# Attention backward on one Trainium2 core: score, dP and dQ matmuls interleaved by head, operands stored by group of heads, and a start flag in place of dQ's memset

## The chip, the cores and the metric

The kernel runs on one core of one Trainium2 chip. The metric is the device time of one execution in microseconds (us); medians of several executions are quoted.

PE is the matmul engine, DVE the vector engine, ACT the activation engine, POOL and SP the two engines that issue most transfers. The kernel uses PSUM as eight banks of 2 KB per partition (its pools take 8 of 8, below); PE writes there, DVE and ACT read from there. The trace records the clock granted to PE: at half clock, matmuls of 512 columns start about 0.41 us apart here in place of 0.215.

## The reference, cut to what matters

One block of a diffusion-style transformer, forward and backward, with S = 2048 tokens, D = 512, and attention with 32 heads of 16.

```python
def _A_ref(x, wqkv, wo):                      # attention
    H = 32; Dh = D // H
    qkv = (x @ wqkv).reshape(B, S, 3, H, Dh).transpose(2, 0, 3, 1, 4)
    q, k, v = qkv[0], qkv[1], qkv[2]
    p = softmax(einsum('bhqd,bhkd->bhqk', q, k) * Dh ** -0.5)
    o = einsum('bhqk,bhkd->bhqd', p, v)
    return o.transpose(0, 2, 1, 3).reshape(B, S, D) @ wo
...
h = layernorm(x) * (1 + ca) + sa
x = x + ga * _A_ref(h, A_wqkv, A_wo)
h = layernorm(x) * (1 + cb) + sb
x = x + gb * mlp(h)                           # squared relu, F = 1792
# outputs: x and the gradients of nine inputs for a given grad_out
```

For each head, the backward pass needs dV = P^T dO', dS = P * (dP - delta), dQ = dS K and dK = dS^T Q, where P is the softmax, recomputed. The kernel divides dO by the softmax sum beforehand (dO') and writes minus delta into padding columns of dO', so that dS is exp(score) times dP as PE delivers it.

## The kernel before: the parts that matter

The heads go in 8 groups of 4, each in 2 pairs. A pair has 4 chunks of 512 keys times 16 blocks of 128 queries: 64 units, 1024 in all. A unit makes two score matmuls, two dP matmuls, two exps, one multiplication (`ds`), and, later, its share of dQ, dK and dV. Every four units one DMA transpose of dS is issued, 256 in all; dQ needs its result two groups later.

```python
stp  = tile_pool(name="p5st", bufs=2, space=PSUM)   # score: 2 banks
dpp  = tile_pool(name="p5dp", bufs=2, space=PSUM)   # dP: 2 buffers of 2 banks
acckv, accq                                         # dK/dV and dQ: 1 bank each, 8 of 8 in use
...
def load_group(g):                                  # operands of the next 4 heads, at the group's turn
    for n, src in {"QT": QTq_d, "dOT": dOTq_d}.items():        # feature-major, 512 KB each
        nc.gpsimd.dma_start(t[:], src[g])
    for n, src in {"K": ktm_d, "Q": qtm_d, "dO": dOp_d}.items():  # token-major, 256 KB each, [S, D] in memory
        nc.gpsimd.dma_start(t[:], src.rearrange("(st p) d -> p st d", p=P)[:, :, g * W:(g + 1) * W])

def dq(u):
    if c == 0 and ib == 0:
        nc.vector.memset(accq[:], 0.0)              # once per pair
    for a in range(2):
        for sub in range(4):
            nc.tensor.matmul(accq[:, ib, a, :], lhsT=dsT[...], rhs=T["K"][...], start=False, stop=False)
    if c == SC - 1 and ib == ST - 1:
        nc.vector.tensor_scalar(d, accq[:], self.scale, None, ALU.mult)   # copy dQ out
...
for i in range(G):                                  # G = 4 units
    for a in range(2): matmul(sts[a], QT, masked KT)           # two scores
    if turnq and i == 3: turn(...)                  # once per pair: dK/dV transposed through a dP buffer
    for a in range(2): matmul(dp[:, a], dOT, masked VT)        # two dP
    for a in range(2): activation(pu[:, a], sts[a], Exp)
    nc.vector.tensor_tensor(dsg[:, i], dp[:], pu[:], ALU.mult)
    if len(pendq) > 2 * G: dq(pendq.pop(0))         # dQ of an earlier unit
    if i == 1: kv_group()                           # dK/dV of four earlier units
nc.sync.dma_start_transpose(dsT[:], dsg[...])
```

The softmax here doesn't subtract the row's maximum and nothing guards it: scores larger than these inputs give would overflow.

Of the kernel before, what the change touches and what calls it, by code (L numbers as in the profile page):

```python
# [33 lines left out]
class K:  # L34
# [29 lines left out]
    def build(self, ctx: ExitStack):  # L64
        tc, nc = self.tc, self.nc
        self.dram_pool = ctx.enter_context(tc.tile_pool(name="dram", bufs=1, space=DRAM))
        self.pp = ctx.enter_context(tc.tile_pool(name="persist", bufs=1))
        S, D, F, H, NQ, ST, DT, FT = self.S, self.D, self.F, self.H, self.NQ, self.ST, self.DT, self.FT
        self.xhat1_d = self.dram("xhat1_d", [S, D], BF16)
        self.qtm_d = self.dram("qtm_d", [S, D], BF16)  # L70
        self.ktm_d = self.dram("ktm_d", [S, D], BF16)
        self.QTq_d = self.dram("QTq_d", [NQ, P, S], BF16)
        self.KTq_d = self.dram("KTq_d", [NQ, P, S], BF16)
        self.VTq_d = self.dram("VTq_d", [NQ, P, S], BF16)
        self.dOTq_d = self.dram("dOTq_d", [NQ, P, S], BF16)
        self.O_d = self.dram("O_d", [S, D], BF16)
        self.O32_d = self.dram("O32_d", [S, D], F32)
        self.xhat2_d = self.dram("xhat2_d", [S, D], BF16)
        self.rT_d = self.dram("rT_d", [FT, P, S], BF16)
        self.duT_d = self.dram("duT_d", [FT, P, S], BF16)  # L80
        self.dx1_d = self.dram("dx1_d", [S, D], F32)
        self.vaug_d = self.dram("vaug_d", [P, ST * H * (DH + 1)], BF16)
        self.dOp_d = self.dram("dOp_d", [S, D], BF16)
        self.dqkv_d = self.dram("dqkv_d", [S, 3 * D], BF16)
        self.dx1b_d = self.dram("dx1b_d", [S, D], BF16)
        self.stash = False
        if self.stash:
            self.put_d = self.dram("put_d", [NQ * 2 * self.SC * ST, P, 2, 512], BF16)

        stop = self.opts.get("stop_after", 99)  # L90
        self.dmaq = [nc.gpsimd]
        self.dmai = 0
        self.open_pools = {}
        phases = [self.phase0, self.phase12, self.phase12b, self.phase3, self.phase4, self.phase45, self.phase5, self.phase6, self.phase7]
        for i, ph in enumerate(phases):
            ph()
            if stop <= i:
                break
        for name in list(self.open_pools)[::-1]:
            self.close_pool(name)  # L100
# [153 lines left out]
    def phase12(self):  # L254
# [8 lines left out]
        with tc.tile_pool(name="p12", bufs=1) as sb, tc.tile_pool(name="p12e", bufs=8) as eb:  # L263
# [11 lines left out]
            qtm_v = self.qtm_d.rearrange("(st p) d -> p st d", p=P)  # L275
            ktm_v = self.ktm_d.rearrange("(st p) d -> p st d", p=P)
# [16 lines left out]
            def tm_group(ps_pool, st, t):  # L293
# [4 lines left out]
                if t < 2:  # L298
# [4 lines left out]
                    dq.dma_start((qtm_v if t == 0 else ktm_v)[:, st, :], ev[:])  # L303
# [76 lines left out]
            with tc.tile_pool(name="p2c", bufs=1) as cp, tc.tile_pool(name="p2q", bufs=2) as qp, \  # L380
# [56 lines left out]
                nc.gpsimd.dma_start(self.O_d.rearrange("(st p) d -> p st d", p=P), O_tm[:])  # L437

# [477 lines left out]
    def step_5a(self, wk, trps, ps, st, dx1_f32):  # L916
# [24 lines left out]
        nc.gpsimd.dma_start(self.dOp_d.rearrange("(st p) d -> p st d", p=P)[:, st, :], dOp_t[:])  # L941
# [133 lines left out]
    def attn_bwd(self):  # L1075
# [11 lines left out]
        with ExitStack() as es:  # L1087
# [20 lines left out]
            def load_group(g):  # L1108
# [5 lines left out]
                for n, src in tm.items():  # L1114
                    t = qp.tile([P, ST, W], BF16, name=f"{n}g")
                    with nc.allow_non_contiguous_dma(reason="128B runs"):
                        nc.gpsimd.dma_start(t[:], src.rearrange("(st p) d -> p st d", p=P)[:, :, g * W:(g + 1) * W])
                    T[n] = t
# [23 lines left out]
            def dq(u):  # L1142
                (T, g, jp, c, ib, i, dsT) = u
                if c == 0 and ib == 0:
                    nc.vector.memset(accq[:], 0.0)
                for a in range(2):
                    col = (2 * jp + a) * DH
                    for sub in range(4):
                        nc.tensor.matmul(accq[:, ib, a, :], lhsT=dsT[:, (i * 2 + a) * 4 + sub, :],  # L1149
                                         rhs=T["K"][:, 4 * c + sub, col:col + DH], start=False, stop=False,  # L1150
                                         skip_group_check=True)
                if c == SC - 1 and ib == ST - 1:
# [14 lines left out]
            turnq = []  # L1167
            with tc.manual_schedule(engines={mybir.EngineType.PE}):
                for g in range(NQ):
                    Tn = load_group(g + 1) if g + 1 < NQ else None  # L1170
                    for jp in range(2):
# [3 lines left out]
                        for c in range(SC):  # L1175
                            c0 = 512 * c
                            for ib0 in range(0, ST, G):
                                dsg = dsp.tile([P, G, 2, 512], BF16, name="ds")
                                for i in range(G):
                                    ib = ib0 + i  # L1180
                                    q = slice(ib * P, (ib + 1) * P)
                                    sts = [stp.tile([P, 512], F32, name="st") for a in range(2)]
                                    for a in range(2):
                                        nc.tensor.matmul(sts[a][:], lhsT=T["QT"][:, q], rhs=masked["KT"][2 * jp + a][:, c0:c0 + 512],  # L1184
                                                         start=True, stop=True)
                                    if turnq and i == 3:
                                        turn(*turnq.pop(0))
                                    dp = dpp.tile([P, 2, 512], F32, name="dp")
                                    for a in range(2):
                                        nc.tensor.matmul(dp[:, a, :], lhsT=T["dOT"][:, q], rhs=masked["VT"][2 * jp + a][:, c0:c0 + 512],  # L1190
                                                         start=True, stop=True)
                                    pu = pup.tile([P, 2, 512], BF16, name="pu")
                                    for a in range(2):
                                        nc.scalar.activation(pu[:, a, :], sts[a][:], ACT.Exp, scale=self.scale)  # L1194
                                    nc.vector.tensor_tensor(dsg[:, i], dp[:], pu[:], ALU.mult)  # L1195
                                    pend.append((T, g, jp, c, ib, kvT, pu, dsg[:, i]))
                                    if len(pendq) > 2 * G:
                                        dq(pendq.pop(0))
# [10 lines left out]
                while pendq:  # L1209
                    dq(pendq.pop(0))  # L1210
# [264 lines left out]
```

## Time and profile before

| | before |
|---|---|
| median of four executions (lowest to highest) | 3472.1 us (3465.1 to 3480.0) |
| attention backward, first to last dS transpose | 1624.1 us |
| median distance of dS transposes | 5.857 us |
| excess: the distances' sum over 255 times the median | 130.5 us |
| PE busy share of the whole span | 87% |

Two views more are worth having. The first is the page's list of costly groups: line, engine, operation, output and inputs, count, busy us, mean ns of one, and the idle time just before them with what ended most of it.

```profile
L1194 ACT ACTIVATE pu<-st 128x512 bf16<-128x512 f32 x2048 | 1101.7, 595 | 508.3 <-PE st L1184 506.5
L1195 DVE TENSOR_TENSOR ds<-dp,pu 128x1024 bf16<-128x1024 f32 x1024 | 1211.0, 1220 | 366.4 <-ACT pu L1194 269.2
L1184 PE MATMUL st<-KTm,QTq 128*128 128x512 bf16 x2048 | 698.5, 384 | 58.2 <-DMA dOTq<-dOTq_d 7.1
L1190 PE MATMUL dp<-VTm,dOTq 128*128 128x512 bf16 x2048 | 617.2, 383 | 0.1
```

ACT and DVE have hundreds of microseconds of idle time here and PE has little, so PE's order is what they wait for. Note the dP matmuls: before the change PE never waited for a dP buffer (0.1 us).

The second view is PE in order of time around a pair boundary (start, length, engine, operation; x2 is two in a row).

```profile
1971.13 0.60 PE L1127 MATMUL acckv<-ds,Qg 128*16 128x512 bf16 x2
1971.52 0.64 PE L1127 MATMUL acckv<-ds,Qg 128*16 128x512 bf16 x2
...
1977.78 0.39 PE L1127 MATMUL acckv<-ds,Qg 128*16 128x512 bf16 x2
1977.99 0.38 PE L1127 MATMUL acckv<-ds,Qg 128*16 128x512 bf16 x2
```

Just after the memset's wait the dK/dV matmuls start about 0.4 us apart; one group later, 0.21. This wait costs its own length and then 3.4 us at half clock. One of the 15 pair boundaries separates the two: at 2998 us the same wait of 2.8 us is followed by full clock, and that boundary loses 2.7 us at the memset, not 4.2.

### The profile page before, as it was taken

Reading aid. Unit: us, or ns where it says so; the run is one execution under the profiler, and the core shown is the slowest. Engines: PE = TensorE matmul, PEld = TensorE weight load, DVE = VectorE, ACT = ScalarE, POOL = GpSimd, SP = SyncE. Lnnn points to the kernel's source line nnn. Section 1 sums busy time; section 2 is a strip of 40 time slices with the busy share of each in tenths; the row PEclk is TensorE's granted clock in tenths of the full one; section 3 lists DMA queues with packets and bytes.
Section 4 is the critical chain, followed back from the end, with each engine's and each line's share of the span. In section 5 each row is a group of like instructions: output and inputs, shape, how many; then the busy total and the mean of one; then the engine's idle time right before and its main releaser. Section 6 shows DMA issues by size and latency. Waiting matters only on the chain. (4 is left out here: it accounts for less than half of the span.)

```text
span 3465.0 us, 75624 instructions
## 1 busy us (share of the span) xinstructions
PE 2998.7 (87%) x31556; PEld 1452.4 (42%) x31556; DVE 1876.3 (54%) x2761; ACT 2350.4 (68%) x3577; POOL 369.9 (11%) x583
## 2 busy tenths in 40 slices
PE   5999998888885968498998989989899998999887
PEld 2445543333332433265443444444344444444433
DVE  6222220000004346364886778878677787887755
ACT  3999999999992324332776667667676676776633
POOL 3111110000002004231101010010101001000000
PEclk8999999999997989699999999999999999999998
DMA  3111110000004365654999999999999999999952
GB/s 123 62 49 50 45 41 12 12 6 12 5 1 164 105 206 196 179 150 117 198 176 172 174 189 178 176 176 175 174 175 184 183 176 176 177 175 172 179 182 66
DMA packets 1178339, 447.82 MB, mean 129 GB/s; under 512 B 1089162, under 2 KB 1145612, under 8 KB 1177996
## 3 DMA queue, kind: packets, MB, share of 16 engines
q1 hardware_dynamic: 1140188, 353.70, 53.1%
q0 software_dynamic: 29184, 79.59, 7.9%
q10 hardware_dynamic: 8624, 9.70, 0.9%
q8 instruction: 247, 4.05, 0.5%
q14 instruction: 96, 0.79, 0.1%
HBM read 106.83 MB, written 67.64 MB: 50 GB/s over the span
## 5 line engine op out<-in xcount | busy, mean ns | idle before, releaser
L1194 ACT ACTIVATE pu<-st 128x512 bf16<-128x512 f32 x2048 | 1101.7, 595 | 508.3 <-PE st L1184 506.5
L1195 DVE TENSOR_TENSOR ds<-dp,pu 128x1024 bf16<-128x1024 f32 x1024 | 1211.0, 1220 | 366.4 <-ACT pu L1194 269.2
L412 ACT ACTIVATE pu<-st 128x1024 bf16<-128x1024 f32 x1024 | 940.1, 1381 | 4.7 <-PE accbank L418 4.7
L1184 PE MATMUL st<-KTm,QTq 128*128 128x512 bf16 x2048 | 698.5, 384 | 58.2 <-DMA dOTq<-dOTq_d 7.1
L1190 PE MATMUL dp<-VTm,dOTq 128*128 128x512 bf16 x2048 | 617.2, 383 | 0.1
L409 PE MATMUL st<-QTm,KTq 128*128 128x512 bf16 x2048 | 606.9, 377 | 6.3 <-ACT pu L412 1.5
L1149 PEld LDWEIGHTS <-dsT 128*128 128x128 bf16 x8192 | 354.4, 96 | 343.1 <-issue 57.1
L418 PEld LDWEIGHTS <-pu 128*128 128x128 bf16 x8192 | 291.9, 96 | 457.9 <-ACT pu L412 407.4
L1149 PE MATMUL accq<-Kg,dsT 128*128 128x16 bf16 x8192 | 356.3, 170 | 92.4 <-DMA dsT<-ds 50.0
L418 PE MATMUL accbank<-Vaug,pu 128*128 128x17 bf16 x8192 | 353.9, 172 | 67.3 <-DVE accbank L405 7.4
L1190 PEld LDWEIGHTS <-dOTq 128*128 128x128 bf16 x2048 | 199.7, 98 | 377.5 <-issue 199.0
L427 DVE RECIPROCAL rl<-accbank 128x4 f32<-128x4 f32 x128 | 23.0, 179 | 526.1 <-PE accbank L418 525.6
L1127 PE MATMUL acckv<-ds,Qg 128*16 128x512 bf16 x2048 | 280.3, 398 | 0.6 <-DVE ds L1195 0.6
L1127 PE MATMUL acckv<-pu,dOg 128*16 128x512 bf16 x2048 | 280.3, 398 | 0.0
L458 POOL DMA_DIRECT2D KTm<-KTq_d x120 | 59.6, 501 | 1151.6 <-PE st L1184 1151.4
L1184 PEld LDWEIGHTS <-QTq 128*128 128x128 bf16 x2048 | 123.0, 96 | 128.9 <-issue 127.3
L288 DVE TENSOR_SCALAR ev_fm<-pps,bcol 128x512 bf16<-128x512 f32 x92 | 69.1, 751 | 195.0 <-PE pps L281 194.0
L409 PEld LDWEIGHTS <-KTq 128*128 128x128 bf16 x2048 | 130.0, 96 | 34.8 <-issue 20.5
L281 PE MATMUL pps<-xhat1T,wpad 128*128 128x512 bf16 x384 | 122.8, 378 | 4.9 <-DVE ev_fm L288 3.8
L1127 PEld LDWEIGHTS <-Qg 128*16 128x16 bf16 x2048 | 75.8, 89 | 73.4 <-issue 12.7
L1127 PEld LDWEIGHTS <-dOg 128*16 128x16 bf16 x2048 | 75.6, 89 | 0.0
L545 ACT ACTIVATE rT<-ups,bias 128x512 bf16<-128x512 f32 x56 | 38.5, 687 | 52.1 <-PE ups L543 52.0
(305 smaller groups left out, 2376.1 us busy)
## 6 DMA issues: line engine op xcount, KB each, us to landing
rT_d<-rT SPq DMA_DIRECT2D x4, 1792.0 KB
rT<-rT_d SPq DMA_DIRECT2D x4, 1792.0 KB
duT_d<-duT POOLq DMA_DIRECT2D x4, 1792.0 KB, 12.9
rT_f<-rT_d SPq DMA_DIRECT2D x14, 512.0 KB
duT_f<-duT_d POOLq DMA_DIRECT2D x14, 512.0 KB, 4.0
xhat_d<-xhat SPq DMA_DIRECT2D x2, 2048.0 KB
QTq_d<-ev_fm POOLq DMA_DIRECT2D x32, 128.0 KB, 2.1
QTm<-QTq_d SPq DMA_DIRECT2D x128, 32.0 KB
```

Of the source, the lines that this page charges most:

```text
L281: nc.tensor.matmul(pt[:, :sw], lhsT=wpads[t][:, kt, g, :], rhs=xhat1T[:, kt, s0:s0 + sw], start=(kt == 0), stop=(kt == DT - 1))
L288: nc.vector.tensor_scalar(ev[:, :sw], pt[:, :sw], bc, None, ALU.add)
L409: nc.tensor.matmul(stt[:, a, :qw], lhsT=KT[:, kb * P:(kb + 1) * P], rhs=QTm[a][:, q0:q0 + qw], start=True, stop=True)
L412: nc.scalar.activation(pu[:, :, :qw], stt[:, :, :qw], ACT.Exp, scale=self.scale)
L418: nc.tensor.matmul(acc[:, a, sub, :], lhsT=pu[:, a, sub * P:(sub + 1) * P], rhs=Vaug[:, kb, heads[a], :], start=False, stop=False, skip_gr ...
L458: eng.dma_start(masked[n][j][r:r + 32, c0:c0 + cw], src[g, r:r + 32, c0:c0 + cw])
L1127: nc.tensor.matmul(acckv[r:r + DH, :], lhsT=T[n][:, ib, col:col + DH], rhs=src[:, a, :], start=(ib == 0), stop=(ib == ST - 1))
L1149: nc.tensor.matmul(accq[:, ib, a, :], lhsT=dsT[:, (i * 2 + a) * 4 + sub, :], rhs=T["K"][:, 4 * c + sub, col:col + DH], start=False, stop=F ...
L1184: nc.tensor.matmul(sts[a][:], lhsT=T["QT"][:, q], rhs=masked["KT"][2 * jp + a][:, c0:c0 + 512], start=True, stop=True)
L1190: nc.tensor.matmul(dp[:, a, :], lhsT=T["dOT"][:, q], rhs=masked["VT"][2 * jp + a][:, c0:c0 + 512], start=True, stop=True)
L1194: nc.scalar.activation(pu[:, a, :], sts[a][:], ACT.Exp, scale=self.scale)
L1195: nc.vector.tensor_tensor(dsg[:, i], dp[:], pu[:], ALU.mult)
```

## The change

The intent has three parts. (1) Each score matmul is followed by the dP matmul of the same head and its part of dQ, so that ACT has time to empty a score bank. (2) The token-major operands K, Q and dO are stored by group of heads, so that a later load reads 2 KB runs in place of 128 B runs; the stores then write 128 B runs. (3) dQ's first matmul of a pair carries a start flag, so the memset, which had to wait for the copy of the pair before, goes; dQ work of the new pair is held back for two units (`hold`), and done in doubles later.

```diff
-        self.qtm_d = self.dram("qtm_d", [S, D], BF16)          # also ktm_d, dOp_d
+        self.qtm_d = self.dram("qtm_d", [NQ, P, ST * 4 * DH], BF16)
...
+    def by_quad(self, t):
+        return t.rearrange("g p (st w) -> p st g w", st=self.ST)
...
-        nc.gpsimd.dma_start(self.dOp_d.rearrange("(st p) d -> p st d", p=P)[:, st, :], dOp_t[:])
+            nc.gpsimd.dma_start(self.by_quad(self.dOp_d)[:, st], dOp_t[:].rearrange("p (g w) -> p g w", g=NQ))
...
-                        nc.gpsimd.dma_start(t[:], src.rearrange("(st p) d -> p st d", p=P)[:, :, g * W:(g + 1) * W])
+                    nc.gpsimd.dma_start(t[:].rearrange("p st w -> p (st w)"), src[g])
...
-                if c == 0 and ib == 0:
-                    nc.vector.memset(accq[:], 0.0)
-                for a in range(2):
+                for a in heads:
...
-                                         rhs=T["K"][:, 4 * c + sub, col:col + DH], start=False, stop=False,
+                                         rhs=T["K"][:, 4 * c + sub, col:col + DH],
+                                         start=(c == 0 and ib == 0 and a == 0 and sub == 0), stop=False,
...
+                                    if len(pendq) > 2 * G:
+                                        if pendq[0][3] == 0 and pendq[0][4] == 0 and hold:
+                                            hold -= 1
+                                        else:
+                                            hold = 2 if pendq[0][4] else 0
+                                            uqs = [pendq.pop(0) for _ in range(2 if len(pendq) > 3 * G - i else 1)]
...
                                     for a in range(2):
+                                        nc.tensor.matmul(stt[:], lhsT=T["QT"][:, q], rhs=masked["KT"][...], start=True, stop=True)
+                                        nc.scalar.activation(pu[:, a, :], stt[:], ACT.Exp, scale=self.scale)
                                         nc.tensor.matmul(dp[:, a, :], lhsT=T["dOT"][:, q], rhs=masked["VT"][...], start=True, stop=True)
+                                        for uq in uqs:
+                                            dq(uq, [a])
```

More of the change, by code (lines that the diff above doesn't have):

```diff
@@ L69, in build @@
         self.xhat1_d = self.dram("xhat1_d", [S, D], BF16)
-        self.qtm_d = self.dram("qtm_d", [S, D], BF16)
-        self.ktm_d = self.dram("ktm_d", [S, D], BF16)
+        self.qtm_d = self.dram("qtm_d", [NQ, P, ST * 4 * DH], BF16)
+        self.ktm_d = self.dram("ktm_d", [NQ, P, ST * 4 * DH], BF16)
         self.QTq_d = self.dram("QTq_d", [NQ, P, S], BF16)
@@ L82, in build @@
         self.vaug_d = self.dram("vaug_d", [P, ST * H * (DH + 1)], BF16)
-        self.dOp_d = self.dram("dOp_d", [S, D], BF16)
+        self.dOp_d = self.dram("dOp_d", [NQ, P, ST * 4 * DH], BF16)
         self.dqkv_d = self.dram("dqkv_d", [S, 3 * D], BF16)
@@ L274, in phase12 @@
             dsts = [self.QTq_d, self.KTq_d, self.VTq_d]
-            qtm_v = self.qtm_d.rearrange("(st p) d -> p st d", p=P)
-            ktm_v = self.ktm_d.rearrange("(st p) d -> p st d", p=P)
+            qtm_v = self.by_quad(self.qtm_d)
+            ktm_v = self.by_quad(self.ktm_d)
             def fm_group(ps_pool, t, g, s0, sw, eng="vector"):
@@ L302, in tm_group @@
                     self.dmai += 1
-                    dq.dma_start((qtm_v if t == 0 else ktm_v)[:, st, :], ev[:])
+                    with nc.allow_non_contiguous_dma(reason="128B runs"):
+                        dq.dma_start((qtm_v if t == 0 else ktm_v)[:, st], ev[:].rearrange("p (g w) -> p g w", g=NQ))
                 else:
@@ L940, in step_5a @@
                                 self.rl[:, st, :].unsqueeze(2).to_broadcast([P, H, DH]), ALU.mult)
-        nc.gpsimd.dma_start(self.dOp_d.rearrange("(st p) d -> p st d", p=P)[:, st, :], dOp_t[:])
+        with nc.allow_non_contiguous_dma(reason="128B runs"):
+            nc.gpsimd.dma_start(self.by_quad(self.dOp_d)[:, st], dOp_t[:].rearrange("p (g w) -> p g w", g=NQ))
         prod = wk.tile([P, H, DH], F32, name="prod")
@@ L1115, in load_group @@
                     t = qp.tile([P, ST, W], BF16, name=f"{n}g")
-                    with nc.allow_non_contiguous_dma(reason="128B runs"):
-                        nc.gpsimd.dma_start(t[:], src.rearrange("(st p) d -> p st d", p=P)[:, :, g * W:(g + 1) * W])
+                    nc.gpsimd.dma_start(t[:].rearrange("p st w -> p (st w)"), src[g])
                     T[n] = t
@@ L1140, in turn, with dq @@
                     nc.scalar.copy(d, v[:, t, :, :, 0:DH])
-            def dq(u):
+            def dq(u, heads):
                 (T, g, jp, c, ib, i, dsT) = u
-                if c == 0 and ib == 0:
-                    nc.vector.memset(accq[:], 0.0)
-                for a in range(2):
+                for a in heads:
                     col = (2 * jp + a) * DH
@@ L1149, in dq @@
                         nc.tensor.matmul(accq[:, ib, a, :], lhsT=dsT[:, (i * 2 + a) * 4 + sub, :],
-                                         rhs=T["K"][:, 4 * c + sub, col:col + DH], start=False, stop=False,
+                                         rhs=T["K"][:, 4 * c + sub, col:col + DH],
+                                         start=(c == 0 and ib == 0 and a == 0 and sub == 0), stop=False,
                                          skip_group_check=True)
-                if c == SC - 1 and ib == ST - 1:
+                if c == SC - 1 and ib == ST - 1 and 1 in heads:
                     h0 = 4 * g + 2 * jp
@@ L1166, in attn_bwd @@
             T = load_group(0)
-            turnq = []
+            turnq, hold = [], 0
             with tc.manual_schedule(engines={mybir.EngineType.PE}):
@@ L1181, in attn_bwd @@
                                     q = slice(ib * P, (ib + 1) * P)
-                                    sts = [stp.tile([P, 512], F32, name="st") for a in range(2)]
-                                    for a in range(2):
-                                        nc.tensor.matmul(sts[a][:], lhsT=T["QT"][:, q], rhs=masked["KT"][2 * jp + a][:, c0:c0 + 512],
-                                                         start=True, stop=True)
+                                    uqs = []
+                                    if len(pendq) > 2 * G:
[4 more added lines that the diff above has]
+                                            uqs = [pendq.pop(0) for _ in range(2 if len(pendq) > 3 * G - i else 1)]
                                     if turnq and i == 3:
@@ L1188, in attn_bwd @@
                                     dp = dpp.tile([P, 2, 512], F32, name="dp")
+                                    pu = pup.tile([P, 2, 512], BF16, name="pu")
                                     for a in range(2):
+                                        stt = stp.tile([P, 512], F32, name="st")
+                                        nc.tensor.matmul(stt[:], lhsT=T["QT"][:, q], rhs=masked["KT"][2 * jp + a][:, c0:c0 + 512],
+                                                         start=True, stop=True)
+                                        nc.scalar.activation(pu[:, a, :], stt[:], ACT.Exp, scale=self.scale)
                                         nc.tensor.matmul(dp[:, a, :], lhsT=T["dOT"][:, q], rhs=masked["VT"][2 * jp + a][:, c0:c0 + 512],
                                                          start=True, stop=True)
-                                    pu = pup.tile([P, 2, 512], BF16, name="pu")
-                                    for a in range(2):
-                                        nc.scalar.activation(pu[:, a, :], sts[a][:], ACT.Exp, scale=self.scale)
+                                        for uq in uqs:
+                                            dq(uq, [a])
                                     nc.vector.tensor_tensor(dsg[:, i], dp[:], pu[:], ALU.mult)
                                     pend.append((T, g, jp, c, ib, kvT, pu, dsg[:, i]))
-                                    if len(pendq) > 2 * G:
-                                        dq(pendq.pop(0))
                                     if i == 1 and len(pend) >= G + 2:
@@ L1209, in attn_bwd @@
                 while pendq:
-                    dq(pendq.pop(0))
+                    dq(pendq.pop(0), [0, 1])
     def phase6(self):
```

## The prediction

> **What bounds the kernel now.** I cut the span by stage first, with the view of busy time in stretches. One stage is over half of it: the backward pass through attention, from 1560 to 3330 us.
>
> ```profile
> 1560.00:3330.00 1770.00, 1596.92 (x17510) 780.02 (x17509) 1319.32 (x1205) 1142.60 (x2101) 157.07 (x279) 0.96 0.98 175
> ```
>
> The columns are the stretch, its length, busy us of PE, PE weight loads, DVE, ACT, POOL, the granted clock, the DMA share and GB/s. PE is busy 90% of it and the DMA engines 98%, so a busy share doesn't say which one sets the end. The whole change lies in this stage, apart from the stores that feed it. I then read the waits inside it, 1700 to 3300 us:
>
> ```profile
> ACT pu L1194 <- PE st L1184: 494.0, 506, 10.2
> DVE ds L1195 <- ACT pu L1194: 256.2, 272, 2.4
> PE accq L1149 <- DMA dsT<-ds: 50.0, 7, 9.8
> PE accq L1149 <- DVE accq L1145: 42.4, 15, 3.0
> ```
>
> PE itself is named with few waits: 50 us for transposed dS to land, once per group of heads, and 42 us for the memset of dQ, once per pair. To see the rest I read one regular group of four units (a unit is one query block of a head pair) in order of time:
>
> ```profile
> 2213.31 0.59 PE L1190 MATMUL dp<-VTm,dOTq 128*128 128x512 bf16 x2
> 2213.74 0.35 PE L1149 MATMUL accq<-Kg,dsT 128*128 128x16 bf16 x8
> 2213.94 0.86 PE L1184 MATMUL st<-KTm,QTq 128*128 128x512 bf16 x2
> 2214.41 4.75 DVE L1195 TENSOR_TENSOR ds<-dp,pu 128x1024 bf16<-128x1024 f32 x4 [1.10 <-ACT pu L1194]
> ...
> 2215.28 0.59 PE L1184 MATMUL st<-KTm,QTq 128*128 128x512 bf16 x2
> ...
> 2216.34 0.86 PE L1184 MATMUL st<-KTm,QTq 128*128 128x512 bf16 x2
> 2216.83 0.31 PEld L1190 LDWEIGHTS <-dOTq 128*128 128x128 bf16 x2 [0.39 <-issue]
> ```
>
> The two score matmuls take 0.59 us in one unit and 0.86 in the next. The 0.27 us more is a wait: there are two score banks, and the second matmul waits until ACT has read its bank. PE counts as busy in it. The groups follow each other every 5.857 us (the median distance between the starts of the 256 dS transposes). PE alone needs 5.31: four units of 1.065 (2215.276 to 2216.341 holds no wait) plus 1.047 for the dK/dV matmuls with their gaps. So PE order and two waits of 0.27 set the pace. The transposes do not:
>
> ```profile
> L1204 SPq DMA_TRANSPOSE dsT<-ds x256: 4764/5042/14930, 1652.0 to 3276.1; - x128
> ```
>
> They run one at a time, 5.04 us in the median, 0.8 less than the period.
>
> The 255 periods sum to 1624.1 us, 130.5 over 255 times the median. Sorted by place, that excess is: about 1.0 us per pair at the turn of dK/dV; 4.2 us at 15 pair boundaries (63 us), where the memset is; and about 9 us more at each of the six boundaries before which a new group's operands load (55 us).
>
> **What the Trainium skill says.** "TensorE: Matmul & The Clock Gate", section "Wait — 56ns, not 53.3ns?", gives 215.7 ns between warm matmuls of 512 columns and a floor near 25 ns for small ones. The trace agrees: 0.215 us for score and dP, 0.0255 for one dQ matmul, weight loads hidden. Its section "What's actually happening" says that PE drops to half clock after an idle window of about 3.4 us. The trace agrees: PE starts nothing for 3.16 us at the memset, and the next dK/dV matmuls come 0.41 us apart, not 0.215. That explains why a wait named at 2.8 us costs 4.2. "PSUM — Partial Sum Buffer", section "The four PSUM rules", says that a first matmul clears the written-bits of its whole 2 KiB bank, and later ones overwrite where the bit is clear. dQ's accumulator is 16 x 2 x 16 floats, one bank, so one start flag can replace the memset; this trace can't show it. "DMA: Bandwidth & Descriptors", section "Specifications", asks for 512 B per transfer for line rate. The trace fits that:
>
> ```profile
> QTq<-QTq_d POOLq DMA_DIRECT2D x6, 512.0 KB, 5.4
> dOTq<-dOTq_d POOLq DMA_DIRECT2D x6, 512.0 KB, 6.9
> ...
> Qg<-qtm_d POOLq DMA_DIRECT2D x6, 256.0 KB, 14.9
> dOg<-dOp_d POOLq DMA_DIRECT2D x6, 256.0 KB, 14.8
> ```
>
> Half the bytes, in 128 B runs, take over twice the time to land. One dS transpose took 14.9 us beside them.
>
> **The change part by part.**
>
> *Interleaving.* No matmul or weight load is added. Each unit becomes score, dP, four dQ matmuls for head 0, then the same for head 1. A half is 0.215 + 0.215 + 4 x 0.0255 = 0.532 us. A score bank is busy 0.412 (matmul start to exp start) + 0.592 (exp) + 0.052 (release) = 1.056 us and is wanted every 2 x 0.532 = 1.064, so both 0.27 us waits go. But dP has two buffers too, and its loop grows. Call D the start of a unit's first dP matmul. Now the second score matmul comes before D, and ds starts 1.10 us after D (2213.306 to 2214.407), runs 1.222 and releases 0.054 later (the latency that PE shows after the memset): 2.38 us. In the new order the second score matmul starts at D + 0.317, so ds starts at D + 0.317 + 0.412 + 0.594 + 0.032 = D + 1.355 and the buffer is free at D + 2.63. The next use is two units on, after 2 x 1.065 = 2.13 us of PE. Where the dK/dV matmuls lie between, nothing waits; where they don't, the first dP waits 0.50. The unit after waits 0.08, because ds follows ds at 1.141 us. New group: 5.31 + 0.58 = 5.89 us, against 5.857. Over 256 groups **+9 us**: a wait on ACT is swapped for a wait on DVE.
>
> *Memset.* 15 boundaries lose 4.2 us. What remains is the copy of dQ out of its bank (0.68 us), which stands on DVE ahead of the last ds of its group. Two units without dQ let it finish; the double ones after them spend that PE time again. I leave 0.6 us: 15 x 3.6 = **-54 us**.
>
> *The turn.* Its transposes take one of the dP buffers, whose loop now binds; I carry the recurrence above through it and get 1.9 us where there was 1.0: 16 x 0.9 = **+14 us**.
>
> *Operand loads.* The bytes stay, in 2 KB runs. The transpose beside the 1 MB of feature-major operands took 8.26 us before the slow ones were at full weight. That delay stays, the next is then 3 us late, and I leave 1.8 us of stall: 6 x (9.2 - 1.8) = **-44 us**.
>
> *Stores.* 32 + 16 stores now write 128 B runs. They lie in stages with the DMA at 10% and about 50%. A POOL issue may rise from 0.5 to the 1.2 us that the strided loads show. Off the path; +2.
>
> Sum: 9 - 54 + 14 - 44 + 2 = -73, so 3473 - 73 = 3400. I put the middle at 3395, as the two costs that I estimated (turn and load stall) are the weakest and on the high side.
>
> **Rivals.** (a) Interleaving pays as it seems meant to: the period falls to PE's 5.31, 256 x 0.55 = 140 us more, near 3255. For it: ACT waits 494 us for score matmuls. Against it: the dP loop above; and DMA transposes of 5.04 us plus the loads would be nearly the next bound. (b) The new dP wait is longer than worked out: 0.1 us more a group is 26 us, and the time is 3420. For it: every step of that loop is taken from the old order, none was seen in the new. (c) The loads were hidden by more than run length: the 1 MB of feature-major operands alone keeps the transposes late, only half the 55 us returns, near 3415. For it: one transpose was 3.2 us late already. (d) Slow stores hold up the dO chain before the stage: some us at most.
>
> **Range and chances.** Most of the gain is two removed stalls that the trace shows as 118 us, of which I keep 98, less 23 for interleaving and turn. An error of 0.1 us in the period is 26 us, and of 2 us in the load stall 12. That gives 3350 to 3432. The 2% line is 3403.5, close to the middle: faster 0.57, same 0.41, slower 0.02.
>
> **What would show it.** The distance of dS transposes near 5.89 us; PE's waits for ACT on st gone, and in their place a wait of the first dP matmul of 0.5 us for ds, once per group; no wait near 3 us on dQ, no half clock at pair boundaries; Qg and dOg landing in under 7 us; no transpose over 10 us. Wrong would be: a period near 5.4 (then dP is released earlier than I think), transposes that stay late at the six boundaries, or a longer stage from 1090 to 1560 us.

## More of the kernel before

The kernel before was timed again beside each set of experiments, with medians from 3471.1 to 3473.5 us, so medians of different sets can be compared to some 3 us; a stage read from a trace is one execution.

In an earlier stage, where dO' is made, its rows are stored by POOL, whose next instruction is the product from which delta comes (16 times, once per block of tokens):

```python
nc.gpsimd.dma_start(self.dOp_d.rearrange("(st p) d -> p st d", p=P)[:, st, :], dOp_t[:])
nc.gpsimd.tensor_tensor(prod[:], dOp, o32[:]..., ALU.mult)
nc.vector.tensor_reduce(nd[:], prod[:], axis=AX.X, op=ALU.add, negate=True)    # minus delta
```

## The result, and the profile after

The changed kernel takes 3432.5 us (median of four, 3426.9 to 3439.2), against 3472.1 before. The ratio is 0.9886, with a 95% interval from 0.9857 to 0.9915: the same within 2%. Ratios here are the mean time of one kernel's runs over that of the other's in the same rounds, so not quite the ratio of the medians quoted. The results are correct, so the start flag does the memset's work, which the prediction's trace could not show. 3395 was predicted, with 3432 as the upper end.

Where the time went, from the two traces:

| us | before | after |
|---|---|---|
| dO stage: its first matmul to the first score matmul of the backward pass | 361.3 | 372.2 |
| first to last dS transpose | 1624.1 | 1573.0 |
| median period of the transposes | 5.857 | 5.892 |
| excess over 255 medians | 130.5 | 70.5 |
| of it at the six boundaries with loads, each | 11.3 to 16.6, sum 85.4 (61.7 without the memset's group) | 6.9 to 10.9, sum 50.9 |
| at a pair boundary without loads | 5.2 | 2.2 |
| half clock between first and last transpose | 102 | 27, all at the six boundaries with loads |

The same stretch for the changed kernel, from 1560 us to 40 us earlier than before at its end (columns as in the prediction):

```profile
1560.00:3290.00 1730.00, 1562.10 (x17603) 778.66 (x17601) 1322.87 (x1221) 1186.79 (x2106) 143.04 (x281) 0.98 0.99 181
```

PE's busy time fell by 35 us with no matmul less, as waits inside matmul records became visible gaps or went, and the granted clock rose from 0.96 to 0.98. The groups of the page and the waits of the stage tell which:

```profile
L1200 ACT ACTIVATE pu<-st 128x512 bf16<-128x512 f32 x2048 | 1143.5, 597 | 411.1 <-PE st L1198 404.3
L1205 DVE TENSOR_TENSOR ds<-dp,pu 128x1024 bf16<-128x1024 f32 x1024 | 1212.5, 1220 | 323.8 <-ACT pu L1200 306.4
L1201 PE MATMUL dp<-VTm,dOTq 128*128 128x512 bf16 x2048 | 778.1, 380 | 102.9 <-DVE ds L1205 101.3
L1198 PE MATMUL st<-KTm,QTq 128*128 128x512 bf16 x2048 | 778.8, 380 | 8.2 <-DMA dOTq<-dOTq_d 7.6
```

```profile
PE dp L1201 <- DVE ds L1205: 101.3, 271, 0.7
PE accq L1151 <- DMA dsT<-ds: 33.0, 7, 6.9
```

In the waits (total us, times, longest) a new line has come: PE waits for DVE before dP matmuls, 271 times, 101 us. The wait of dQ for its memset, 42.4 us before, is gone. One regular group, PE and DVE in order of time, shows the new wait in place:

```profile
2218.48 0.39 PE L1198 MATMUL st<-KTm,QTq 128*128 128x512 bf16 x1
2218.70 0.38 PE L1201 MATMUL dp<-VTm,dOTq 128*128 128x512 bf16 x1
2218.92 0.25 PE L1151 MATMUL accq<-Kg,dsT 128*128 128x16 bf16 x4
2219.03 0.38 PE L1198 MATMUL st<-KTm,QTq 128*128 128x512 bf16 x1
...
2220.62 0.38 PE L1198 MATMUL st<-KTm,QTq 128*128 128x512 bf16 x1
2221.34 0.38 PE L1201 MATMUL dp<-VTm,dOTq 128*128 128x512 bf16 x1 [0.35 <-DVE ds L1205]
```

A half unit takes 0.55 us (2218.48 to 2219.03; 0.53 in the later units), and no score matmul waits for ACT. At 2220.62 a score matmul starts, and the dP matmul that should follow 0.215 later starts 0.72 later: a wait of 0.50, the length that the prediction gave. It is the third unit after the dK/dV matmuls, where two units of PE are shorter than the loop of a dP buffer.

At a boundary with loads, this is PE:

```profile
2063.37 0.38 PE L1201 MATMUL dp<-VTm,dOTq 128*128 128x512 bf16 x1 [0.35 <-DVE ds L1205]
2069.20 0.28 PE L1151 MATMUL accq<-Kg,dsT 128*128 128x16 bf16 x4 [5.45 <-DMA dsT<-ds]
2069.33 0.59 PE L1198 MATMUL st<-KTm,QTq 128*128 128x512 bf16 x1
2069.71 0.63 PE L1201 MATMUL dp<-VTm,dOTq 128*128 128x512 bf16 x1
```

dQ waits 5.45 us for a transpose, and then score and dP start 0.38 apart in place of 0.22: half clock again. The tile view of the transposes in this stretch (min, median and max ns, first and last start), then the stage's transposes and the loads of Q and dO at the six boundaries (median us to landing, from 1700 to 3290 us):

```profile
L1212 SPq DMA_TRANSPOSE dsT<-ds x2: 5071/10118/15165, 2051.1 to 2066.4; - x2
```

```profile
L1212 SPq DMA_TRANSPOSE dsT<-ds x256: 4766/5049/16257, 1665.1 to 3238.1; - x128
```

```profile
Qg<-qtm_d POOLq DMA_DIRECT2D x6, 256.0 KB, 11.7
dOg<-dOp_d POOLq DMA_DIRECT2D x6, 256.0 KB, 11.9
```

The loads now have 2 KB runs, and yet Q and dO take 11.7 and 11.9 us (14.9 and 14.8 before), and one transpose per boundary 12.2 to 16.3 us. What the queues moved in 6 us of that stall and in 6 us of a regular group (packets, MB, share of 16 engines' time; q1 carries the transposes, q0 the loads that POOL issues):

```profile
q1 hardware_dynamic: 1046, 0.27, 77.4%
q0 software_dynamic: 158, 0.44, 39.4%
```

```profile
q1 hardware_dynamic: 3993, 1.01, 101.5%
```

The first is 2060 to 2066 us, the second 2216 to 2222. Beside 0.44 MB of loads the transposes moved 0.27 MB in place of 1.01, and both together did less (117 GB/s) than the transposes alone (173 GB/s). The packet records show where: most 4 KB load packets took as long as ever (median 0.17 us from 2057 to 2067 us; 0.16 from 2052 to 2056, when the Q^T and dO^T loads moved and the transpose, though issued, hardly did), but 24 of these 128 took over 1 us, up to 2.0, against none of the earlier 254.

### The profile page after: what moved, and what is told of

It reads as the page before. It is cut to its first block, busy times and chain, and to the rows that moved or that the text cites. A ratio compares the mean times of both kernels' runs of the same rounds, so it can differ in the third digit from the quotient of the medians.

```text
span 3427.8 us, 75641 instructions
## 1 busy us (share of the span) xinstructions
PE 2957.0 (86%) x31556; PEld 1444.9 (42%) x31556; DVE 1877.4 (55%) x2745; ACT 2392.2 (70%) x3577; POOL 372.7 (11%) x583
## 5 line engine op out<-in xcount | busy, mean ns | idle before, releaser
L1200 ACT ACTIVATE pu<-st 128x512 bf16<-128x512 f32 x2048 | 1143.5, 597 | 411.1 <-PE st L1198 404.3
L1201 PE MATMUL dp<-VTm,dOTq 128*128 128x512 bf16 x2048 | 778.1, 380 | 102.9 <-DVE ds L1205 101.3
L1198 PE MATMUL st<-KTm,QTq 128*128 128x512 bf16 x2048 | 778.8, 380 | 8.2 <-DMA dOTq<-dOTq_d 7.6
L1151 PEld LDWEIGHTS <-dsT 128*128 128x128 bf16 x8192 | 488.4, 96 | 650.9 <-issue 203.1
L1151 PE MATMUL accq<-Kg,dsT 128*128 128x16 bf16 x8192 | 493.6, 170 | 33.0 <-DMA dsT<-ds 33.0
L1131 PE MATMUL acckv<-ds,Qg 128*16 128x512 bf16 x2048 | 267.0, 382 | 0.8 <-DVE ds L1205 0.7
L1131 PE MATMUL acckv<-pu,dOg 128*16 128x512 bf16 x2048 | 267.0, 382 | 0.0
L1198 PEld LDWEIGHTS <-QTq 128*128 128x128 bf16 x2048 | 196.0, 96 | 134.5 <-issue 131.2
L288 DVE TENSOR_SCALAR ev_fm<-pps,bcol 128x512 bf16<-128x512 f32 x92 | 69.1, 751 | 195.5 <-PE pps L281 194.6
```

Of the source, the lines that this page charges most:

```text
L288: nc.vector.tensor_scalar(ev[:, :sw], pt[:, :sw], bc, None, ALU.add)
L1131: nc.tensor.matmul(acckv[r:r + DH, :], lhsT=T[n][:, ib, col:col + DH], rhs=src[:, a, :], start=(ib == 0), stop=(ib == ST - 1))
L1151: nc.tensor.matmul(accq[:, ib, a, :], lhsT=dsT[:, (i * 2 + a) * 4 + sub, :], rhs=T["K"][:, 4 * c + sub, col:col + DH], start=(c == 0 and i ...
L1198: nc.tensor.matmul(stt[:], lhsT=T["QT"][:, q], rhs=masked["KT"][2 * jp + a][:, c0:c0 + 512], start=True, stop=True)
L1200: nc.scalar.activation(pu[:, a, :], stt[:], ACT.Exp, scale=self.scale)
L1201: nc.tensor.matmul(dp[:, a, :], lhsT=T["dOT"][:, q], rhs=masked["VT"][2 * jp + a][:, c0:c0 + 512], start=True, stop=True)
```

## The experiments

All are edits of the changed kernel. "Stage" is first to last dS transpose.

### Each part of the change undone

**e1_pair_order.** Scores of both heads, then both dP, then dQ, as before; the rest as in the changed kernel.

```diff
                                     for a in range(2):
                                         ...score, exp...
+                                    for a in range(2):
                                         ...dP...
-                                        for uq in uqs:
-                                            dq(uq, [a])
+                                    for uq in uqs:
+                                        dq(uq, [0, 1])
```

> The changed kernel with the interleaving undone alone (both scores, both dP, then dQ of both heads). Theory (the dP buffers bind in the interleaved order, so interleaving swaps a wait on ACT for one on DVE): the period of the dS transposes goes back from 5.89 to about 5.86 us, the turn gets a little cheaper, and the time falls by 10 to 20 us against the changed kernel, near 3415 to 3422. Rival (interleaving is worth its 0.5 us a group and something else holds the kernel up): the time rises by 50 us or more.

Measured: 3409.8 us (3408.9 to 3412.4), ratio 0.9822 (0.9803 to 0.984) to the kernel before; period 5.855, stage 1558.0. So the interleaving by itself costs about 22 us (0.9886 less 0.9822, of 3472), a little more than expected. Of that 15 lie in the stage: 9 in the period (255 x 0.037) and 6 at the boundaries; in the traces 3 us more lie before the dO stage and 2 after the last transpose, where the code is the same and runs differ by as much.

**e2_rows_back.** The three operands in rows again, stored and loaded as before; interleaving and start flag kept.

> The changed kernel with the three token-major operands stored and loaded as before (whole rows out, 128 B runs in). Prediction's reading: the stalls at the six group boundaries grow by 7 us each, the time rises by about 44 us. New reading after the profile: the boundaries lose only 2 to 3 us each more than now, and the stages before the attention backward pass get some 8 us shorter, so that the time stays within 10 us of 3432.

Measured: 3435.0 us (3425.9 to 3439.4), ratio 0.989 (0.9867 to 0.9913), so no different from the changed kernel. But the parts moved: the dO stage is 362.3 us again (372.2 in the changed kernel), and the six load boundaries sum to 69.1 (50.9). The new storage gains 18 us where it loads and pays 10 where it stores. The 18 is good to some 5 us: e12 and e14 below, with the loads of the changed kernel, have sums of 54.6 and 55.7.

**e3_memset_back.** The memset for each pair, no start flag, no hold.

> The changed kernel with the memset of dQ's bank back in place of the start flag and without the two-unit hold. If the memset is what cost 4.2 us at each of 15 pair boundaries: the excess there returns, 2 to 4 us each, the time rises by 20 to 60 us. If the boundary cost was only the order of the copy on DVE: no rise.

Measured: 3470.4 us (3466.4 to 3474.0), ratio 0.9995 (0.9971 to 1.0019); stage 1614.8, a pair boundary without loads about 5.0 us (2.2 without memset). So dropping the memset is worth 38 us of time, 42 in the stage, and is about all that the whole change gains (40 us). The wait for the memset is shorter in this order than in the kernel before, where it was 42.4 us:

```profile
PE accq L1153 <- DVE accq L1149: 29.1, 15, 1.9
```

It still costs more than its length: PE starts no matmul for 2.3 us, and half clock follows at 11 of the 15 boundaries.

**e12_no_hold.** dQ of a new pair not held back (`hold` stays 0).

> The changed kernel without the two-unit hold of dQ at a pair boundary. By the worked-out chain the copy of dQ's bank fits beside waits that are there anyway: excess at odd boundaries within 0.3 us of the 2.2 us of now. If the hold is what took the memset's place: 1 us or more at each boundary.

One run: 3431.0 us, a pair boundary without loads 2.2 as before it. Holding back two units buys nothing that shows, so, as far as one run can tell, the 38 us of e3, which dropped the hold too, are the memset's.

### The wait of dP

**e4_short_dp.** The order score, dQ, score, dQ, dP, dP: no score matmul stands between the first dP and the second, and the loop of a dP buffer is short again.

```diff
                                     for a in range(2):
                                         ...score, exp...
-                                        ...dP...
                                         for uq in uqs:
                                             dq(uq, [a])
+                                    for a in range(2):
+                                        ...dP...
```

> The changed kernel with dP's two matmuls moved behind the second score matmul (score, dQ, score, dQ, dP, dP). dP is then written 0.3 us nearer to its use, the buffer's loop is shorter, and the score matmuls are still apart. Theory: the period falls to about 5.65 us, the time by 55 to 65 us against the changed kernel, near 3370, unless the transposes (5.05 us one at a time) and their stalls at the boundaries take some of it back. Rival (the wait of dP for ds is not what sets the period): the period stays within 0.05 of 5.89.

Measured: 3384.9 us (3379.9 to 3388.4), ratio 0.9748 (0.9727 to 0.9768); period 5.670, stage 1534.8. The line of PE waiting for ds before dP has all but gone:

```profile
PE dp L1204 <- DVE ds L1206: 4.9, 15, 0.5
```

255 x 0.222 would be 57 us; the stage got 38 shorter, because the excess at boundaries rose from 70.5 to 88.9. PE is faster, the transposes are not, and so the load stalls are felt more.

**e8_split_kv.** dK/dV not once per four units but in two halves, after the second and the fourth.

```diff
-                for u in pend[:G]:
+                for u in pend[:G // 2]:
...
-                                    if i == 1 and len(pend) >= G + 2:
+                                    if i % 2 == 1 and len(pend) >= G + 2:
```

> The changed kernel with the dK/dV matmuls of four units issued two and two, after the second and the fourth unit, not all after the second. Theory (the dP buffer's loop of 2.63 us against two units of 2.13 us is broken only where dK/dV matmuls lie between): now half of them lie between every second pair of units, so that the wait shrinks from 0.58 to about 0.1 us a group; the second entry costs about 0.2 us of its own gaps. Period about 5.57 us, time down by 75 to 90 us against the changed kernel before what the transposes take back, 3345 to 3375. Rival (the period is set elsewhere): it grows by the 0.2 us of gaps, time up by 50 us.

Measured: 3340.4 us (3335.6 to 3347.5), ratio 0.9622 (0.96 to 0.9643); period 5.558, stage 1488.8. No matmul was taken away; 92 us came from where the same eight dK/dV matmuls stand. Now each pair of units has half of them in between, so each dP buffer gets 2.13 + 0.52 us, about its loop of 2.63. The wait:

```profile
PE dp L1201 <- DVE ds L1205: 9.8, 30, 0.5
```

### The loads at the group boundaries

**e5_no_token_loads** and **e6_no_feature_loads** give wrong results (relative errors of 1.4 and 1.5 in one output): groups after the first reuse the first one's K, Q and dO (e5), or its Q^T and dO^T (e6), so part of the loads is gone (0.75 MB of the 1.75 per group in e5, 1 MB in e6).

> The changed kernel without the token-major loads of K, Q and dO after the first group of heads (wrong results on purpose: the first group's tiles are used again). It asks what is left of the boundary stalls, 8.5 us each with 2.1 of the turn in it. If the token-major loads still cause them though their runs are now 2 KB: the six boundaries fall to about 2 to 3 us each, and no transpose takes over 10 us. If the 1 MB of feature-major operands causes them: they stay above 6 us.

> The changed kernel without the feature-major loads of Q and dO after the first group (wrong results on purpose). If these 1 MB make the transposes late, the boundaries fall to about 2 to 3 us each. If the token-major loads beside a transpose in flight are the cause, they stay above 5 us, and the loads of Q and dO still take over 7 us to land.

Measured, one run each: 3387.9 and 3383.6 us. In both, the six load boundaries fall to what any pair boundary costs (2.2 us; one at 2.8), and no transpose is over 10 us (e5, then e6):

```profile
L1215 SPq DMA_TRANSPOSE dsT<-ds x256: 4757/5018/9574, 1663.4 to 3199.3; - x128
```

```profile
L1215 SPq DMA_TRANSPOSE dsT<-ds x256: 4742/5018/6314, 1659.6 to 3194.9; - x128
```

So neither set of loads stalls PE alone; a delay of some microseconds fits in the slack that dQ has, two groups later, and only both together exceed it. Together they also cost more than the sum: the two transposes nearest to a load boundary run over the median by 3.5 us with Q^T and dO^T alone, by 0.7 with K, Q and dO alone, and by 9.2 with both (10.9 in the kernel before). Without Q^T and dO^T ahead of them, Q and dO land in 6 to 7 us:

```profile
Qg<-qtm_d POOLq DMA_DIRECT2D x6, 256.0 KB, 6.1
dOg<-dOp_d POOLq DMA_DIRECT2D x6, 256.0 KB, 7.0
```

**e13_loads_in_queue** puts the next group's five loads into the queue of the transposes (issued by SP in place of POOL), where they stand between transposes; the order on SP was left to the scheduler, which put Q^T and dO^T before one transpose, Q and dO after it. **e7_spread_sync** fixes SP's order too, one load after every second transpose.

```diff
-                    Tn = load_group(g + 1) if g + 1 < NQ else None
+                    Tn = {}
...
                                 nc.sync.dma_start_transpose(dsT[:], dsg[...])
+                                slot = 4 * c + ib0 // G - 4
+                                if jp == 0 and g + 1 < NQ and slot % 2 == 0 and 0 <= slot < 10:
+                                    load_one(g + 1, Tn, ("QT", "dOT", "K", "Q", "dO")[slot // 2])   # nc.sync.dma_start
```

> The changed kernel with the operand loads in the transposes' queue as in the spread version, but not spread: they stay where they are in the changed kernel, two feature-major loads, a transpose, Q and dO, two transposes, K. If the queue alone is what helped (no load meets a transpose in flight): the boundaries fall to about 2 to 3 us each and the time is near 3392. If the spacing helped (the delays of one boundary come together and use up the slack): the boundaries stay at 5 us or more, the time above 3410.

> The changed kernel with each group's five operand loads issued one at a time, two groups of blocks apart, in the queue of the transposes and behind one of them, so that no load comes while a transpose is in flight from another queue and no two loads follow each other. If stalls come from loads that meet a transpose in flight or from all five coming together: the six boundaries fall to about 2 us each, the time by some 35 us, near 3395. If the mere bytes (1.75 MB per group of heads) are what the transposes can't absorb: the stalls move to where the loads now are and the time stays.

Measured: e13 3393.0 us (3391.3 to 3394.1), ratio 0.978 (0.9765 to 0.9795); e7 3390.0 us (3389.0 to 3390.7), ratio 0.9764 (0.9749 to 0.9778). The transposes of e13 and of e7:

```profile
L1221 SPq DMA_TRANSPOSE dsT<-ds x256: 4630/5008/8789, 1662.7 to 3201.0; - x128
```

```profile
L1221 SPq DMA_TRANSPOSE dsT<-ds x256: 4673/5086/7172, 1662.2 to 3199.4; - x128
```

The same bytes in the same runs: the excess over the stage is 35.9 us in e13 and 34.3 in e7, against 70.5 in the changed kernel, and neither trace has any half clock in the stage. So moving the loads to the transposes' queue took away 34.6 of the 36.2 us, and spreading them 1.6. (In e13 the transposes come 3.7 us late at a load boundary, but 1.0 us of that is made good in the groups that follow.) Both runs change two things at once: the loads share the transposes' queue, and they are issued by SP in place of POOL. Which of the two it is was not tested; loads from a third engine's queue would tell.

### The store of dO

**e14_store_sp.** Only the store of dO is issued by SP in place of POOL.

```diff
-            nc.gpsimd.dma_start(self.by_quad(self.dOp_d)[:, st], ...)
+            nc.sync.dma_start(self.by_quad(self.dOp_d)[:, st], ...)
```

> The changed kernel with nothing but the store of dO issued from SP's queue. If POOL's issue of that store is what made the stages before longer: 361 to 363 us from the first matmul of the layer norm's backward pass to the first score matmul, against 372 in the changed kernel and 361 before, with the same boundaries as the changed kernel, and a time near 3422.

Measured: 3422.6 us (3421.1 to 3429.5), ratio 0.9871 (0.9849 to 0.9892); the dO stage 362.4 us, against 372.2 in the changed kernel and 361.3 before. The times alone overlap by a little; the stage's length is clear. The store in the kernel before, and in the changed one (the issuing engine's ns, min, median, max):

```profile
L941 POOL DMA_DIRECT2D dOp_d<-dOp_t x16: 540/540/552, 1294.0 to 1447.3; - x16
```

```profile
L946 POOL DMA_DIRECT2D dOp_d<-dOp_t x16: 895/906/906, 1296.2 to 1455.7; - x16
```

POOL is occupied 0.37 us longer by each of 16 issues, 5.9 us in all, and its next instruction is the product from which delta comes, which the rest of the stage waits for. The starts of the 16 products bear this out: in the regular blocks they follow each other every 8.88 us before, 9.24 in the changed kernel and 8.10 in e14, and from first to last they take 153.3, 159.5 and 151.7 us. The other 4 us of the stage's growth lie after the last product, up to the first score matmul (195.7 before, 199.9 in the changed kernel, 198.9 in e14); I did not find their cause, and e14 makes up for 2 of them by leaving POOL free before.

### Together

**e9_split_spread** joins e8 and e7. **e10_split_spread_rows_dO** is e9 with dO stored in rows and loaded in 128 B runs. **e11_split_spread_store_sp** is e9 with the store of dO issued by SP.

> The changed kernel with both earlier edits: dK/dV matmuls in two halves, and operand loads one at a time in the transposes' queue. If the two gains are of two causes they add: period 5.56 us, boundaries about 2.2 us each, 3432 - 92 - 42 = about 3298. If the shorter period leaves the transposes (5.05 us of every 5.56) too little room for the loads: the period holds, but the groups after a load are late, and the time stays above 3315.

> As the last, with dO alone stored by rows again and loaded in 128 B runs. It asks where the 8 to 10 us come from that the stages before the attention backward pass are longer by. If it is the store of dO in 128 B runs, in the chain of each block: the time from the first matmul of the layer norm's backward pass to the first score matmul falls from about 372 us to about 362, the whole by the same or, if the 128 B load costs stalls, by less. If it is the stores of Q and K: it stays at 372.

> As the one before, with dO stored by groups of heads (128 B runs), but issued from SP's queue, not from POOL's. If the 0.37 us more that POOL spends on each issue of that store (0.91 against 0.54), ahead of its product in the same queue, is the cost: the stages before fall by 8 to 10 us as with rows. If it is the landing of small runs in memory: no change.

Measured: e9 3318.9 us (3318.1 to 3325.2), ratio 0.9566 (0.9549 to 0.9583). The two gains don't add: boundaries are at 2.2 us as in e7, but over the twelve groups in which the loads go out the transposes come 21 us late in sum (2 us in e7), and the median period is 5.582 against 5.558. With the period at 5.58 a transpose of 5.2 us leaves about 0.4 us per group for a load's share of the queue; e7 had 0.8.

e10 3316.9 us (3311.8 to 3320.7), ratio 0.9552: the dO stage is back to 360.9, with Q and K still stored by group, so it is dO's store that made it longer; but the stage is 13 us longer (1479.5 against 1466.3) with the strided load in the queue. A draw with e9.

e11 3309.0 us (3306.4 to 3316.6), ratio 0.9534 (0.9516 to 0.9552): dO stage 361.0, stage 1466.0. It beats both kernels, by 163 us the one before and by 124 the changed one.

## Why the prediction was wrong

The median was 3432.5, 37 us above the prediction. Taken by the steps of its sum:

- **Interleaving (+9): right.** The period is 5.892, predicted 5.89, so 255 x 0.035 = +9. The 0.5 us wait of the first dP for ds stands where it was worked out, `ds` starts 1.37 us after the first dP matmul in the median (worked out: 1.355), and it is the rival's 140 us of gain that did not come (rival a). e1, e4 and e8 confirm it from three sides: the loop of a dP buffer, applied to their orders, had given 5.65 for e4 and 5.57 for e8 ahead of their runs, and 5.670 and 5.558 were measured.
- **Memset and turn (-54 + 14 = -40): right.** Before, the excess outside the load stalls was 130.5 - (61.7 - 6 x 1.0) = 74.8. After, it is 70.5 - (50.9 - 6 x 2.2) = 32.8, so -42. That counts 1.0 us of a turn before as the prediction does, and for after the 2.2 us of a boundary without loads, for turn and copy (1.9 and 0.6 in the prediction). No half clock is left at these boundaries, as foretold.
- **Operand loads (-44): the step that failed.** "In 2 KB runs" was to make Q and dO land in under 7 us, with "1.8 us of stall" left at each boundary. Measured: the load stall went from 55.7 us to 50.9 - 6 x 2.2 = 37.7, so -18, and Q and dO landed in 11.7 and 11.9 us. The sum left at a boundary only the delay of the Q^T and dO^T loads, read from one transpose of 8.26 us, the first of six (8.3 to 14.6 in that trace), and counted Q and dO in 2 KB runs as costing the transposes nothing. The first half held: with Q^T and dO^T alone (e5) the transposes there take 5.7 to 9.6 us. The second failed: with Q and dO beside them they take 12.2 to 16.3. I had put the slow landing down to the 128 B runs, because a view of the kernel before showed short runs and slow landing together. They came together with a second thing: in that kernel Q and dO are the loads that are still moving when the next transpose starts. e2 shows the runs' own share (18 us at six boundaries); e13 and e7 show the rest, with the runs as they are. The prediction's rival (c), near 3415, comes nearest, and it had too little weight. It named the wrong load, however: Q^T and dO^T alone make the transposes a little late but stall nothing (e5); both sets in one row do.
- **Stores (+2, "Off the path"): wrong.** They cost 10.9 us in the dO stage, and e14 takes 10 of it back by moving one issue to another engine. The prediction foresaw that the issue gets longer (0.54 to 0.91 us; it said that 0.5 "may rise" to 1.2) but did not look at what POOL does next. Rival (d) had named this chain with "some us at most".

The two failed terms are 26 and 9 us, 35 of the 36 by which the sum of -73 missed the profiled spans (3465.0 to 3427.8, -37). A further 3 us of the changed kernel's trace lie outside both stages (2 before, 1 after), where runs of the same code differ by as much, and the -2 of memset and turn stands against it. Two of the signs that the prediction named for being wrong came: transposes late at the six boundaries, and a longer stage before 1560 us. The shading from 3400 down to 3395 rested on turn and load stall being on the high side; for the load stall it was the low side.

What stays open: why some load packets take up to 2.0 us beside a transpose, which of the two waits for the other inside the DMA engines, whether the shared queue or the issuing engine is what helps in e13 and e7, and the 4 us after the last product of the dO stage.

## What to carry to other kernels

Before matmuls are reordered, work out for every PSUM buffer the time from its first write to its last reader's end in the new order, and hold it against PE's time between two uses: giving one pair of buffers room can shorten another's, and where filler matmuls stand (e8, 92 us) can matter more than the interleaving itself (22 us lost). When two explanations of a slow transfer appear together in one profile, such as short runs and a neighbour in flight, an estimate that removes one of them should keep the other at full size. And an issue that gets dearer counts in full where the issuing engine's next instruction is on the path: move the issue first.

## What the Trainium skill lacked or had wrong

- "DMA: Bandwidth & Descriptors", section "Rules for kernel authors", says of correctness that a transpose next to ordinary DMAs needs nothing, and that spreading DMAs over issuing engines doesn't help bandwidth. It lacks the cost in time: in the changed kernel a transpose beside loads from POOL's queue took 12.2 to 16.3 us where the median is 5.05, 24 of one boundary's 128 load packets over 1 us where the median is 0.17, and the same loads in the transposes' own queue took 40 us off the kernel (e13, e7; longest transpose 8.8 and 7.2 us; issuing engine and queue changed together). That both could share a queue with profit is on no page.
- Same page, section "Specifications": the 512 B for line rate is no guide to landing time beside other traffic. Going from 128 B to 2 KB runs changed the landing of Q and dO from 14.9 and 14.8 to 11.7 and 11.9 us only; taking away the loads ahead of them gave 6.1 and 7.0 (e6).
- Same page, section "Anatomy of one DMA — SWDGE (gpsimd) path": it calls descriptor generation small and variable, and says that many descriptors can be emitted before the incremental cost shows. Here POOL's issue went from 0.54 us to 0.91 when the same 128 KB were written in 128 B runs, and about 6 us of that came onto the path (16 issues of 0.37 us more; e14).
- "TensorE: Matmul & The Clock Gate", section "What's actually happening", gives an idle window of about 3.4 us before half clock. The kernel before shows half clock after 3.2 us without a matmul start at its memset (the prediction called that agreement), and e3 after 2.3 us at 11 of 15 boundaries, so a shorter gap can be enough. The 215.7 ns and the floor near 25 ns in the page's section "Wait — 56ns, not 53.3ns?" agree with the traces (0.215 us and 0.0255 us).
- No page has a way to work out the loop of a double-buffered PSUM tile, which added 0.5 us or more to PE's own time in each group of the kernels before and after: matmul start to the dependent exp's start 0.412 us, and 0.05 us from the end of ACT's or DVE's read to PE's next write.
